# Pooled attention by couples of head pairs in 64x64 quadrants, the fifth local unit turned by DMA, in a fused attention and SoLU feed-forward kernel

## The chip, the cores and the metric

The kernel runs on one core of a Trainium2 chip. The time is the device time of one execution in microseconds (us); the time of a kernel is the median of its timed runs. A profile is taken in an execution of its own.

## The reference, cut to what matters

Eight batches of eight heads, 576 positions, 64 numbers a head. Two attentions are added: one over sequences pooled by 4 (144 positions), repeated four times, and one within a band of 3 positions to either side. Then comes a feed-forward layer with SoLU and a layer norm, over all 4608 positions.

```python
q_d = q.reshape(B, H, Sd, factor, D).mean(axis=3)        # k_d, v_d alike
out_up = np.repeat(sm_attn(q_d, k_d, v_d), factor, axis=2)
mask = np.abs(pos[:, None] - pos[None, :]) < factor
scores = np.where(mask, scale * np.matmul(q, k.transpose(0, 1, 3, 2)), -1000000000.0)
out_local = np.matmul(softmax(scores), v)
x = (out_up + out_local).transpose(0, 2, 1, 3).reshape(B * S, H * D)
h = x @ w_in                                             # 512 -> 1024
e = np.exp(h - h_max)
solu = h * e / (e.sum(-1) + 1e-9)
ln = (solu - mu) / np.sqrt(var + 1e-06) * g_ln
return ln @ w_out                                        # 1024 -> 512
```

## The kernel before

The work is cut into steps. Each piece is a generator (`steps`, `pair_steps`, `ffn_in`, ...) whose parts between two `yield`s are one step each. `plan` lists all steps, 2029 of them, and the list ORDER (lines 26 to 123) says in which order they are written into the program; the engines then run their instructions in that order, each in its own queue, and wait for each other by semaphores. A second list, OTHER, names steps whose element-wise operation goes to the other of two engines. All DMAs are issued by SyncE (SP), in order.

**Attention, a batch at a time.** q and k are loaded and turned to have the head's 64 numbers on partitions (two heads above each other: a pair of heads, four pairs). They are summed by four for the pooled attention (`sums`, line 418).

- *Local attention* takes ten windows of 64 positions, two of them in a unit, five units a batch. The scores `sc` (lines 607, 695) and the products with the values `xp` (lines 665, 753) are matmuls of 64 rows by 64 columns of the array. Between the two the weights have to be turned. `Local` does it on TensorE (`plt`, line 655) and copies the result out of PSUM (line 658). `PairOfLocals`, for batches 3 to 7 and units 0 to 3, does it by eight DMAs in blocks of 32 rows (`plT<-pl`, line 741) and a DVE transpose within blocks of 32 (line 746). Unit 4 is a `Local` in every batch.
- *Pooled attention* (`Pooled`, line 773) takes one pair of heads at a time. Scores `sd` (line 788) are six matmuls of 64 rows, 64 columns and 144 moving columns. The softmax runs over three thirds of 48 queries. `pdt` (line 823) turns the weights in twelve TensorE transposes, 64 rows by 72 columns; two copies take them out of PSUM (`pdT`, lines 830 and 833). `po` (line 844) are four matmuls with 72 keys on the rows. The result is added to x four times over (`accumulate`, line 574). The pooled values `vd` are summed from four loads of 72 rows by two additions each (`pooled_vsum`, line 484).

**Feed-forward, 36 tiles of 128 positions.** x is split into a high and a low part (`xh`, `xl`, `xhl`, line 1009); `ffn_in` multiplies with the split w_in (24 matmuls of 128x512, `h`, line 862), takes the maximum, the exponential, the product, the mean and the scale s (lines 870 to 926) and sends the result to DRAM (`u`); `ffn_back` reads it back in blocks, DVE turns it (`v`, line 963), ACT and POOL or DVE split it (`uh`, `ul`), and `ffn_out` makes the other 24 matmuls (`o`, line 990). These wide matmuls stand between the small ones of attention, wherever ORDER puts them.

Of the kernel before, what the change touches and what calls it, by code (L numbers as in the profile page):

```python
# [10 lines left out]
F32 = mybir.dt.float32  # L11
# [24 lines left out]
124 126 417 133 134 213 214 125 143 215 239 506 113 114 288 240 241 429 430 289 431 432 663 264  # L36
155 248 486 225 418 2 487 493 494 135 136 226 495 227 290 313 156 228 229 291 230 440 242 243
496 21 244 245 231 419 246 422 292 441 137 442 249 507 293 294 488 489 497 490 653 144 145 247
5 462 250 451 433 265 463 420 251 148 464 465 23 423 295 296 256 297 252 298 314 315 4 266 267
253 428 268 254 255 452 461 443 316 9 257 466 302 453 317 146 147 157 158 269 318 319 434 258  # L40
338 17 339 435 436 473 474 421 658 513 514 19 475 467 272 259 299 340 300 515 454 437 444 476
270 654 271 438 260 664 261 468 262 445 477 469 303 304 305 439 363 341 342 343 498 499 263 470
446 447 455 306 307 456 471 320 321 659 344 309 280 281 648 665 660 273 472 655 656 457 458 322
364 478 282 365 301 479 661 500 283 666 459 284 448 285 366 460 480 274 286 449 287 275 345 481
276 277 424 426 327 278 279 649 482 650 651 308 501 502 508 346 347 509 689 510 690 516 691 491
492 677 678 701 323 702 668 679 425 427 324 325 310 311 517 348 680 349 713 328 329 330 331 332
652 518 519 326 511 512 367 333 681 520 714 682 334 335 521 368 369 676 352 688 336 725 674 522
523 692 736 683 684 370 371 13 350 524 881 737 715 525 372 657 716 703 704 312 738 662 373 353
354 526 726 355 356 359 357 685 358 360 686 693 351 694 886 548 527 727 695 705 377 746 573 706
528 696 529 887 530 888 687 531 747 549 378 379 717 361 700 718 667 1139 728 889 550 551 532  # L50
533 697 698 374 669 552 882 707 891 748 375 598 675 739 599 380 381 699 766 876 767 553 719 708
554 709 768 384 710 711 574 769 892 337 756 740 555 883 884 556 537 382 383 670 557 712 923 362
562 672 893 720 757 894 741 742 743 758 877 724 534 376 535 940 900 671 770 878 879 729 575 576
577 578 880 385 386 538 579 539 885 540 541 580 542 906 907 908 909 730 910 731 911 581 582 600
721 601 912 913 558 387 759 760 543 544 545 559 1122 560 561 761 762 763 941 563 564 536 732
583 584 914 942 924 1127 733 925 926 927 915 565 566 602 546 587 890 744 567 568 749 750 928
734 623 722 603 904 1132 604 673 569 570 735 723 745 1123 751 1124 585 605 929 752 753 606 607
608 609 624 764 765 952 571 930 943 944 945 946 947 771 754 755 772 588 589 625 773 626 627 590
591 592 774 628 775 776 777 547 972 953 916 954 629 630 1117 973 594 610 778 901 895 931 586
1128 779 962 917 611 593 780 974 932 948 801 949 631 595 963 781 826 975 782 802 803 1125 964  # L60
804 783 612 955 922 956 632 633 1133 896 965 966 967 596 613 614 918 615 634 635 616 617 1129
933 934 1134 968 1135 805 1118 806 969 636 807 618 919 597 619 620 1130 905 572 935 902 784
1119 1120 982 983 984 920 897 921 827 828 985 637 950 638 639 621 903 951 898 936 1131 640 899
829 830 937 938 939 976 977 986 970 978 979 971 785 641 642 957 958 1165 980 959 1166 1167 808
786 1338 787 981 1168 809 643 987 790 1169 1170 1121 988 788 960 831 961 644 989 1147 832 1148
1149 1150 833 834 990 991 1171 1151 1152 851 1017 852 1333 791 1126 810 811 812 813 814 1193
1182 1334 792 1172 793 645 1173 1146 646 853 1335 1339 854 1348 1136 622 992 1018 815 794 795
797 855 647 1141 856 1153 857 816 817 835 1340 796 798 818 1194 993 994 789 836 1343 858 859
837 799 819 820 1183 821 1349 838 1184 1154 1195 1344 995 996 997 840 860 1137 822 823 1174
1175 1345 1346 998 1163 1138 865 841 842 843 1196 999 1042 1203 1336 839 800 1213 1214 1215  # L70
1204 1350 1341 861 1351 866 1143 1216 1155 1019 1020 1021 1156 1140 1157 1000 1001 1181 824 844
1205 845 846 1176 862 1363 1364 863 864 1067 1365 1584 1366 1367 1022 847 848 1574 1023 1398
1399 1381 867 1382 1217 1043 1044 1185 1068 1045 1337 868 869 849 1024 1144 1186 1187 1025 1368
1177 1178 1188 1400 1369 1383 1401 1206 1026 1207 850 1002 1027 1189 1384 1092 1046 1164 870
1003 1004 871 1370 1047 1385 1218 1028 1223 1352 1048 872 873 1006 1145 1219 1220 1069 1347
1208 1224 1158 1225 1159 1031 1386 1226 1070 1209 1210 1029 874 1007 1008 1049 1009 1160 1161
1361 1190 1032 1162 1191 1192 825 1197 1211 1227 1228 1371 1342 1142 1589 1093 1071 1010 1179
1180 1013 1011 1012 1372 1014 1033 1387 1034 1035 1229 1230 1030 1072 1212 1073 1050 1409 1362
1355 1373 1198 1231 1074 1199 1575 1075 1410 1411 1005 1051 1015 1585 1076 1056 1077 1094 1095
1402 1232 1200 1586 1587 1221 1412 1374 1375 1388 1222 1096 1376 1419 1036 1201 1439 1389 1202  # L80
# [1079 lines left out]
```

## Time and profile before

| | |
|---|---|
| timed runs (us) | 582.44, 582.76, 589.12; median 582.76 |
| span of the profiled execution | 587.5 us |
| granted TensorE clock, mean | 0.990 |
| busy: PE, DVE, ACT, POOL | 568.1, 472.5, 333.4, 298.9 us |
| DMA | 99.59 MB, q1 65.7% of 16 engines' time |

PE is TensorE's matmuls, PEld its weight loads, DVE is VectorE, ACT ScalarE, POOL GpSimd, SPq the queue of SyncE that issues DMAs. A name such as `pdt<-ident,pd` says which tile an instruction writes and which it reads. A form such as `64*72 64x64` says how many rows and columns of the array a matmul uses, and then the partitions and elements that it works on. A row of the timeline has the start and the length in us; the note in brackets is the idle time before it and what ended it. A busy time is the time in which any instruction of the group ran; since matmuls are pipelined, the length of one is more than its distance to the next. In groups by line, the columns are the busy time, the mean of one in ns, and the engine's idle time before, with what released it.

### The profile page before, as it was taken

Reading aid. Unit: us, or ns where it says so; the run is one execution under the profiler, and the core shown is the slowest. Engines: PE = TensorE matmul, PEld = TensorE weight load, DVE = VectorE, ACT = ScalarE, POOL = GpSimd, SP = SyncE. Lnnn points to the kernel's source line nnn. Section 1 sums busy time; section 2 is a strip of 40 time slices with the busy share of each in tenths; the row PEclk is TensorE's granted clock in tenths of the full one; section 3 lists DMA queues with packets and bytes.
Section 4 is the critical chain, followed back from the end, with each engine's and each line's share of the span. In section 5 each row is a group of like instructions: output and inputs, shape, how many; then the busy total and the mean of one; then the engine's idle time right before and its main releaser. Section 6 shows DMA issues by size and latency. Waiting matters only on the chain.

```text
span 587.5 us, 15257 instructions
## 1 busy us (share of the span) xinstructions
PE 568.1 (97%) x5852; PEld 437.2 (74%) x5852; DVE 472.5 (80%) x779; ACT 333.4 (57%) x750; POOL 298.9 (51%) x447
## 2 busy tenths in 40 slices
PE   7899989999999997999999999999999999999997
PEld 3676667777777775877777777777777777788875
DVE  7999999899898878897988876898879777644650
ACT  4788678468546644466475653457545664453452
POOL 3767588857373744358543455357431842433130
PEclk9999999999999996999999999999999999999999
DMA  8999767788877888577867887665666245314221
GB/s 279 288 218 229 169 140 183 196 183 172 220 160 183 187 197 181 154 167 180 180 152 198 222 197 192 155 192 152 177 190 133 91 142 164 113 44 167 89 91 54
DMA packets 207113, 99.59 MB, mean 170 GB/s; under 512 B 163136, under 2 KB 193344, under 8 KB 207040
## 3 DMA queue, kind: packets, MB, share of 16 engines
q1 hardware_dynamic: 207040, 98.61, 65.7%
q8 instruction: 46, 0.75, 0.6%
q14 instruction: 27, 0.22, 0.1%
HBM read 65.54 MB, written 27.79 MB: 159 GB/s over the span
## 4 chain that ended last, share of the span: by engine, by line
PE 72%; DVE 13%; DMA 4%; POOL 4%; ACT 3%; issue 2%; SPq 0%; DVEq 0%; ACTq 0%; POOLq 0%
PE o L990 30%; PE h L862 28%; PE po L844 2%; PE sc L695 2%; PE sd L788 2%; DMA v<-u 2%; PE xp L753 2%; PE pdt L823 2%; PE sc L607 1%; DVE nmx L870 1%; DVE w L375 1%; DVE e L877 1%; DMA vs<-in_v_dram 1%; PE plt L655 1%; DVE w L379 1%
## 5 line engine op out<-in xcount | busy, mean ns | idle before, releaser
L862 PE MATMUL h<-wi_h,xh 128*128 128x512 f32 x288 | 116.9, 406 | 1.4 <-DVE e L877 1.3
L990 PE MATMUL o<-wo_h,uh 128*128 128x512 f32 x288 | 117.4, 408 | 0.4 <-ACT osb L997 0.4
L862 PE MATMUL h<-wi_h,xl 128*128 128x512 f32 x288 | 114.4, 397 | 0.7 <-POOL xl L1024 0.7
L990 PE MATMUL o<-wo_l,uh 128*128 128x512 f32 x288 | 114.6, 398 | 0.0
L862 PE MATMUL h<-wi_l,xh 128*128 128x512 f32 x288 | 113.7, 395 | 0.0
L990 PE MATMUL o<-wo_h,ul 128*128 128x512 f32 x288 | 79.0, 396 | 0.0
L973 POOL TENSOR_TENSOR ul<-v,uh 128x512 fp32r<-128x512 f32 x40 | 51.8, 1296 | 43.6 <-ACT uh L970 35.5
L874 ACT ACTIVATE e<-h,nmx 128x1024 f32<-128x1024 f32 x36 | 40.1, 1114 | 47.1 <-DVE nmx L870 43.4
L862 PEld LDWEIGHTS h<-wi_h,xh 128*128 128x128 f32 x288 | 54.1, 188 | 16.7 <-issue 2.9
L990 PEld LDWEIGHTS o<-wo_h,uh 128*128 128x128 f32 x288 | 54.6, 189 | 15.8 <-issue 1.4
L862 PEld LDWEIGHTS h<-wi_h,xl 128*128 128x128 f32 x288 | 54.1, 188 | 15.3 <-POOL xl L1024 2.1
L990 PEld LDWEIGHTS o<-wo_h,ul 128*128 128x128 f32 x288 | 54.1, 188 | 13.4 <-DVE ul L973 0.3
L990 PEld LDWEIGHTS o<-wo_l,uh 128*128 128x128 f32 x288 | 54.7, 190 | 12.2
L870 DVE TENSOR_REDUCE nmx<-h 128x1 f32<-128x1024 f32 x36 | 43.7, 1215 | 24.8 <-PE h L862 24.8
L862 PEld LDWEIGHTS h<-wi_l,xh 128*128 128x128 f32 x288 | 54.1, 188 | 12.0
L877 DVE SCALAR_TENSOR_TENSOR e<-h,e 128x1024 f32<-128x1024 f32 x36 | 43.8, 1216 | 14.8 <-ACT e L874 14.7
L970 ACT ACTIVATE uh<-v 128x512 fp32r<-128x512 f32 x70 | 42.7, 624 | 20.7 <-issue 8.5
L963 DVE STREAM_TRANSPOSE v<-v 128x512 f32<-128x512 f32 x70 | 46.4, 688 | 4.2 <-DMA v<-u 4.1
L997 ACT ACTIVATE osb<-o,s 128x512 f32<-128x512 f32 x36 | 24.5, 681 | 40.4 <-PE o L990 24.8
L1024 POOL TENSOR_TENSOR xl<-x,xh 128x512 fp32r<-128x512 f32 (+1 forms) x26 | 32.6, 1256 | 22.3 <-ACT xh L1021 22.0
L487 POOL TENSOR_TENSOR vs<-vs 72x512 f32<-72x512 f32 x24 | 31.6, 1318 | 17.0 <-DMA vs<-in_v_dram 16.7
L882 POOL TENSOR_SCALAR nmu<-su 128x1 f32<-128x1 f32 x36 | 8.2, 228 | 59.8 <-DVE e L877 56.9
(128 smaller groups left out, 1124.0 us busy)
## 6 DMA issues: line engine op xcount, KB each, us to landing
u<-e SPq DMA_DIRECT2D x35, 512.0 KB
v<-u SPq DMA_DIRECT2D x140, 128.0 KB
vs<-in_v_dram SPq DMA_DIRECT2D x32, 288.0 KB
out_dram<-osb SPq DMA_DIRECT2D x36, 256.0 KB
qm<-in_q_dram SPq DMA_DIRECT2D x96, 72.0 KB
km<-in_k_dram SPq DMA_DIRECT2D x96, 72.0 KB
vw<-in_v_dram SPq DMA_DIRECT2D x80, 64.0 KB
vw<-in_v_dram SPq DMA_DIRECT2D x40, 128.0 KB
```

The source lines that it names most:

```text
L487: eng.tensor_tensor(out=vs[:, :, 0:2 * D], in0=vs[:, :, 0:2 * D], in1=vs[:, :, 2 * D:4 * D], op=ALU.add)
L695: nc.tensor.matmul(at[rows(wi), par, pr], bt.qT[rows(par), pr, s0:s0 + W], bt.kT[rows(par), pr, s0:s0 + W], start=True, stop=True,)
L862: nc.tensor.matmul(hps[:, n, :], src[:, cc, :], wt[:, cc, n * 512:(n + 1) * 512], start=(cc == 0 and src is xh and wt is wi_h), stop=(cc = ...
L870: nc.vector.tensor_reduce(out=nmx, in_=hf, op=ALU.max, axis=AX.X, negate=True)
L874: nc.scalar.activation(e, hf, AF.Exp, bias=nmx, scale=1.0, accum_out=se)
L877: nc.vector.scalar_tensor_tensor(out=e, in0=hf, scalar=1.0, in1=e, op0=ALU.mult, op1=ALU.mult, accum_out=su)
L963: nc.vector.transpose(vg, vg)
L970: nc.scalar.activation(uh, tp, AF.Copy)
L973: (usual if v is None else engine(usual, nc.vector)).tensor_tensor(out=ul, in0=tp, in1=uh.bitcast(F32), op=ALU.subtract)
L990: nc.tensor.matmul(o, src[:, j, :], wt[:, 4 * g + j, :], start=(g == 0 and j == 0 and src is uh and wt is wo_h), stop=(g == 1 and j == 3 a ...
L997: nc.scalar.activation(osb, o, AF.Copy, scale=s)
L1024: engine(nc.gpsimd, nc.vector).tensor_tensor(out=l, in0=src, in1=h.bitcast(F32), op=ALU.subtract)
```

## The change

The first 470 steps of ORDER stay. From there on both lists are new (the plan has 1868 steps), and four things change in what the steps do.

1. From batch 2 on (`COUPLED = 2`) `Couple` takes the place of `Pooled`: two pairs of heads, g and g + 2, are done together. Scores are twelve matmuls, as many as two pairs had, in an order that goes round all four quadrants of the array. The weights are turned by 36 plain matmuls with the identity, 48 x 48, instead of 2 x 12 transposes. po has three thirds of 48 keys, twelve matmuls of 48 rows instead of 2 x 4 of 72. Both pdT copies and both additions to x become one for two pairs. Values are loaded in three pieces of 112 rows, the heads 0 to 3 on the lower half and 4 to 7 on the upper.
2. Unit 4 of batches 3 to 7 is turned by eight DMAs and a DVE transpose like the other units: `PairOfLocals` becomes `ByTransfers`, for one unit or two.
3. From tile 7 on (`SHORT = 7`) the scale s of the layer norm is worked out from the sum of exponentials directly: one POOL operation more, three fewer, and no reciprocal on DVE.
4. Code for a way of summing values on TensorE, which was switched off, is gone.

```diff
+    COUPLED = 2
+    SHORT = 7
...
+    class Couple:
+        def steps(self):
+            prs = (g, g + 2)
+            sd = two_banks(*scores_bank(b, g), f"sd_{b}_{g}")[:, :, 0:QC * SD]
+            at = sd.rearrange("p a (c n) -> p a c n", c=QC)
+            for c in range(QC):
+                for a, pr in enumerate(prs):
+                    for par in range(2):
+                        nc.tensor.matmul(
+                            at[rows(par ^ a), a, c, :],
+                            qd_flat[rows(par), (NPR - 1 - pr) * SD + c * QN:][:, 0:64],
+                            bt.kd[rows(par), pr, :], start=True, stop=True,
+                        )
...
+            for k in range(KC):
+                for c in range(QC):
+                    for x, a in TILES:
+                        q_rows = slice(x * 64, x * 64 + QN)
+                        nc.tensor.matmul(
+                            to[a * 64:a * 64 + KN, x, k, c, :],
+                            pds[a][q_rows, c, k * KN:(k + 1) * KN], ident[q_rows, q_rows],
+                            start=True, stop=True,
+                        )
...
+            for k in range(KC):
+                for a in range(2):
+                    for par in range(2):
+                        keys = slice(a * 64, a * 64 + KN)
+                        nc.tensor.matmul(
+                            po[rows(par), a, :], bt.vd[keys, k, 2 * g + par, :],
+                            pdT[keys, par ^ a, k, :], start=k == 0, stop=k == KC - 1,
+                        )
...
+        if i >= SHORT:
+            nc.gpsimd.tensor_scalar(
+                out=se, in0=se, scalar1=se, scalar2=1e-6, op0=ALU.mult, op1=ALU.mult
+            )
...
+        if i >= SHORT:
+            m2 = small.tile([P, 1], F32, tag="m2", name=f"m2_{i}")
+            nc.scalar.activation(e0, e, AF.Square, accum_out=m2)
+            yield
+            nc.gpsimd.tensor_scalar(
+                out=m2, in0=m2, scalar1=1.0 / DFF, scalar2=se, op0=ALU.mult, op1=ALU.add
+            )
+            nc.gpsimd.tensor_tensor(out=s, in0=m2, in1=mhalf, op=ALU.pow)
...
-            local = [PairOfLocals(bt, 0, not late), PairOfLocals(bt, 2, not late), Local(bt, 4, not late)]
-        pooled = [Pooled(bt, pr, late) for pr in range(NPR)]
+            local = [
+                (ByTransfers(bt, u, n, not late), 16 if n == 2 else 12, range(u, u + n))
+                for u, n in ((0, 2), (2, 2), (4, 1))
+            ]
+        if bt.b < COUPLED:
+            pooled = [(Pooled(bt, pr, late), 10, ()) for pr in range(NPR)]
+        else:
+            pooled = [(Couple(bt, g), 12, ()) for g in range(2)]
```

How the two orders differ on TensorE after 768 wide matmuls (16 tiles' worth; batches 4 and 5 are under way). Before:

```order
L862 MATMUL h_4788<-wi_h,xl_4392 128x512
L844 MATMUL po_2_4820<-pdT_2_4428,vd_4025 64x144 x4
L753 MATMUL xp_0_4828<-plT_0_4681,vw_0_4583 64x64 x16
L788 MATMUL sd_1_4853<-kd_3810,qd_flat 64x144 x6
L844 MATMUL po_0_4863<-pdT_0_4747,vd_4025 64x144 x4
L788 MATMUL sd_3_4868<-kd_3810,qd_flat 64x144 x6
L990 MATMUL o_4951<-wo_h,uh_0_4700 128x512
```

Three kinds of small group alternate, and po (72 rows by 64 columns) uses the array in another form than xp and sd (64 by 64). In the changed kernel, at the same place and 24 wide matmuls earlier:

```order
L892 MATMUL pdt_1_4658<-ident,pd_1_0_4480 48x48 x2
L892 MATMUL pdt_1_4658<-ident,pd_1_1_4484 48x48 x2
L892 MATMUL pdt_1_4658<-ident,pd_1_0_4480 48x48
L912 MATMUL po_0_4695<-pdT_0_4489,vd_4326 64x144 x12
L930 MATMUL h_4729<-wi_h,xh_4491 128x512
...
L847 MATMUL sd_1_4759<-kd_4019,qd_flat 64x144 x12
L912 MATMUL po_1_4772<-pdT_1_4713,vd_4326 64x144 x12
```

One sd and one po now hold what two held, all of these groups lie within 64 by 64, and no group of another form stands between them. On SP, in the first batch that turns by DMA (batch 3), before:

```order
L741 DMA plT_0_2801<-pl_0_2573 32x512 x4
L286 DMA qm_2687<-in_q_dram 32x18x32 x4
L286 DMA km_2688<-in_k_dram 32x18x32 x4
L942 DMA v_3232<-u_2945 32x4x256 x4
L299 DMA vw_2_3239<-in_v_dram 64x8x64 x2
L910 DMA u_3243<-e_3039 128x1024
L316 DMA vs_0_0_3248<-in_v_dram 72x4x256
```

And now:

```order
L718 DMA plT_0_2970<-pl_0_2403 32x512 x4
L296 DMA vs_1_3077<-in_v_dram 64x4x256
L296 DMA vs_1_3077<-in_v_dram 48x4x256
L718 DMA plT_4_3080<-pl_110 32x256 x4
L1081 DMA out_dram<-osb_3052 128x512
L1024 DMA v_3168<-u_2966 32x4x256 x4
L982 DMA u_3229<-e_2978 128x1024
L718 DMA plT_4_3080<-pl_110 32x256 x4
```

The turning of unit 4 (`plT_4`) has moved into this queue, four issues for each of the two windows, among the loads of the values (`vs`, now two issues a piece) and the round trip of the feed-forward tiles (`u`, `v`).

More of the change, by code (lines that the diff above doesn't have):

```diff
@@ L225, in pooled_local_attention_then_solu_ffn @@
     nc.vector.memset(mhalf, -0.5)
-    GR = SD // 2
-    BAND = {0: (0, 16), 1: (3, 15), 3: (1, 15)}
-    bands = {}
-    def make_bands():
-        t = moe.tile([P, DFF], F32, tag="e", name="bands")[:, 0:3 * 160]
-        t = t.rearrange("p (r x) -> p r x", r=3)
-        nc.gpsimd.memset(t, 0.0)
-        by_half = ident.rearrange("p (h k) -> p h k", h=2)
-        for n, (r, (off, m)) in enumerate(BAND.items()):
-            nc.vector.tensor_reduce(
-                out=t[:, n, GR:GR + m],
-                in_=by_half[:, :, off:off + FAC * m].rearrange("p h (j i) -> p j h i", i=FAC),
-                op=ALU.add, axis=AX.XY,
-            )
-            bands[r] = t[:, n]
     LP = 2 * W + 2
@@ L312, in big, with load_halves @@
         return load.tile([P, 1024], F32, tag="big", name=name, bufs=6)
+    def load_halves(b, c):
+        vs = big(f"vs_{b}_{c}").rearrange("p (h x) -> p h x", h=H // 2)
+        for half, n in ((0, 64), (1, KN)):
+            src = v[b, half * (H // 2), c * KN * FAC, :]
+            nc.sync.dma_start(
+                vs[half * 64:half * 64 + n],
+                bass.AP(
+                    tensor=src.tensor, offset=src.offset,
+                    ap=[[FAC * D, n], [S * D, H // 2], [1, FAC * D]],
+                ),
+            )
+        return vs[0:ROOM]
     def load_vs(b, c, hs):
@@ L734, in steps @@
             yield
-            plT = big(f"plT_{b}_{u}")
+            if units == 2:
+                plT = big(f"plT_{b}_{u}")
+            else:
+                plT = wk.tile([P, NPR, 2, W], F32, tag="plT", name=f"plT_{b}_{u}")
+                plT = plT.rearrange("p r a w -> p (r a w)")
             half = N * 32
@@ L747, in steps @@
             yield
-            plT = plT.rearrange("p (a n h q) -> p n h a q", a=2, n=2, q=32)
-            for n in range(2):
+            plT = plT.rearrange("p (a n h q) -> p n h a q", a=2, n=units, q=32)
+            for n in range(units):
                 xp = two_banks(ps_a, "a", f"xp_{b}_{u + n}")
@@ L841, in steps @@
                 for par in range(2):
-                    parts = bt.value(kc, 2 * pr + par)
-                    for n, vt in enumerate(parts):
-                        nc.tensor.matmul(
-                            po[par * 64:par * 64 + 64, :], vt, pdT[:, kc, par * SD:(par + 1) * SD],
-                            start=(kc == 0 and n == 0), stop=(kc == 1 and n == len(parts) - 1),
-                        )
+                    nc.tensor.matmul(
+                        po[rows(par), :], bt.vd[:, kc, 2 * pr + par, :],
+                        pdT[:, kc, par * SD:(par + 1) * SD], start=kc == 0, stop=kc == 1,
+                    )
             yield
@@ L1057, in tile_in @@
         row(xhl(i), 2)
-        row(ffn_in(i), 12 if i not in ON_PE else 11)
+        row(ffn_in(i), (12 if i < SHORT else 10) - (i in ON_PE))
         if i not in ON_PE:
```

161 lines of the change are left out of this document (98 added, 63 removed), and 173 rows, old and new, of tables (ORDER, OTHER).

## The prediction

> **What bounds the kernel now.** I read the page first: the busy shares and the chain that ended last.
>
> ```profile
> span 587.5 us, 15257 instructions
> PE 568.1 (97%) x5852; PEld 437.2 (74%) x5852; DVE 472.5 (80%) x779; ACT 333.4 (57%) x750; POOL 298.9 (51%) x447
> PE 72%; DVE 13%; DMA 4%; POOL 4%; ACT 3%; issue 2%; SPq 0%; DVEq 0%; ACTq 0%; POOLq 0%
> ```
>
> TensorE is the bound by its share, but a share says nothing of stages. So next I asked for busy time in stretches, cut where the granted clock changes (columns: length, then PE, PEld, DVE, ACT and POOL busy with instruction counts, clock, DMA share, GB/s).
>
> ```profile
> 104.00:222.00 118.00, 116.18 (x1204) 89.50 (x1196) 102.17 (x166) 68.58 (x161) 70.81 (x104) 1.00 0.80 186
> 222.00:226.00 4.00, 1.14 (x22) 0.78 (x20) 4.00 (x5) 2.78 (x5) 2.06 (x4) 0.79 0.76 180
> 226.00:235.00 9.00, 8.97 (x102) 7.03 (x103) 7.03 (x11) 3.29 (x7) 2.49 (x4) 0.52 0.94 190
> 246.00:584.00 338.00, 336.41 (x2850) 264.30 (x2848) 252.79 (x407) 175.75 (x391) 152.00 (x257) 1.00 0.56 152
> ```
>
> PE idles 1.8 us in the first row, 2.9 in the second and 1.6 in the last: 6.3 us in all from 104 us on. The rest is matmul work. So a microsecond taken from PE is a microsecond of the end, as long as the others keep up. Rows two and three are one accident. At 0.79 of the clock for 4 us and 0.52 for 9 us, 4 x 0.21 + 9 x 0.48 = 5.2 us of clock were lost, and this came behind PE's longest wait:
>
> ```profile
> 220.03 3.79 DVE L490 TENSOR_TENSOR vd<-vs 72x256 f32<-72x256 f32 x1
> ```
> ```profile
> 226.03 0.38 PE L695 MATMUL sc<-kT,qT 64*64 64x64 f32 x4 [2.90 <-DVE pdT L265]
> ```
>
> A sum of values took 3.79 us on DVE, the copy of pdT behind it came late, and PE stood for 2.90 us. The span is 587.5 us and the median of the timed runs 582.76 us; the span less the 5.2 us of lost clock is 582.3 us. I take it that the timed median holds no half clock, and sum from 582.4 us.
>
> **The change part by part.** All its PE work is small matmuls between the wide ones, so their prices are wanted. In the timeline a group's price is the distance from its start to the next group's start. The form reads rows*columns of the array, then out rows x moving columns.
>
> ```profile
> 356.07 0.69 PE L753 MATMUL xp<-plT,vw 64*64 64x64 f32 x32
> 356.59 0.64 PE L665 MATMUL xp<-plT,vw 64*64 64x56 f32 x32
> 357.16 0.49 PE L990 MATMUL o<-wo_h,uh 128*128 128x512 f32 x1
> ```
> ```profile
> 428.04 0.60 PE L655 MATMUL plt<-ident,pl 128*128 128x128 f32 x4
> 428.57 0.53 PE L823 MATMUL pdt<-ident,pd 64*72 64x64 f32 x12
> 429.03 0.69 PE L753 MATMUL xp<-plT,vw 64*64 64x64 f32 x32
> 429.65 0.50 PE L990 MATMUL o<-wo_h,uh 128*128 128x512 f32 x1
> ```
>
> The same 32 records of xp cost 0.52 us where a group of the same 64*64 form follows, 0.57 where the form was there already but a full-width matmul follows, and 0.62 where both neighbours have another form. So entering a form costs 0.05 us, leaving it 0.10, and the work 0.47. A visit to a form costs 0.15 us. The 32 records are 16 matmuls of the program (each plain fp32 matmul stands as two records, the transposes of pdt as one). 16 matmuls in 0.47 us are eight steps of two, 0.058 us a step: the two halves of the rows work at once, two quadrants at a time and not four. And 56 columns cost no less than 64.
>
> ```profile
> 316.29 0.71 PE L844 MATMUL po<-pdT,vd 72*64 72x144 f32 x8
> 316.93 0.69 PE L753 MATMUL xp<-plT,vw 64*64 64x64 f32 x32
> ...
> 318.04 0.71 PE L844 MATMUL po<-pdT,vd 72*64 72x144 f32 x8
> 318.68 0.71 PE L788 MATMUL sd<-kd,qd_flat 64*64 64x144 f32 x12
> 319.32 0.50 PE L990 MATMUL o<-wo_h,uh 128*128 128x512 f32 x1
> ```
> ```profile
> 263.99 1.20 PE L788 MATMUL sd<-kd,qd_flat 64*64 64x144 f32 x24
> 265.12 0.50 PE L862 MATMUL h<-wi_h,xh 128*128 128x512 f32 x1
> ```
>
> po (four matmuls, 72 rows, so no halves) costs 0.64: less the visit 0.49, or 0.122 us for a matmul of 144 columns. sd (six matmuls) costs 0.64, less the visit 0.49; two of them in a row 1.13, less the visit 0.98. That is eight steps of 0.122 for twelve matmuls, where perfect pairs would need six.
>
> Now the sum, 24 pairs of heads (batches 2 to 7) against 12 couples:
> - Scores sd: 24 x 0.49 = 11.8 us. A couple's twelve matmuls alternate the halves of the rows in the order that sc and xp have, so I take six steps: 12 x 6 x 0.122 = 8.8. Saved 3.0 (nothing, if they take eight).
> - Turning pdt: 0.46 (428.57 to 429.03), less the visit 0.31; 24 x 0.31 = 7.4. A couple has 36 plain matmuls of 48 columns in alternating quadrants, 18 steps at 0.058: 12 x 1.04 = 12.5. Lost 5.1.
> - Values po: 24 x 0.49 = 11.8. A couple has twelve matmuls of 144 columns, but in the order of rows low, low, high, high. No group of before has that order. Bounds: six steps as in sc (8.8) and twelve, one after the other, as in po now (17.6). Nearest is sd, which also repeats a half and needs eight: 12 x 8 x 0.122 = 11.7. Saved 0.1, with -5.8 to +3.0 as the ends.
> - Turning the last local unit on PE goes in batches 3 to 7:
>
> ```profile
> 91.47 0.60 PE L655 MATMUL plt<-ident,pl 128*128 128x128 f32 x4
> 91.82 0.48 PE L862 MATMUL h<-wi_h,xh 128*128 128x512 f32 x1
> ```
>   0.35 us each, 5 x 0.35 = 1.8 saved.
> - Forms: pdt and po each had a form of their own (64*72, 72*64); now every small group but the plt has 64*64. I counted the visits in the order of PE from where the two orders part: 109 before, 49 after. 60 x 0.15 = 9.0 saved. This is the largest term, and none of it stands in the change's arithmetic.
>
> In all 3.0 - 5.1 + 0.1 + 1.8 + 9.0 = 8.8 us less on PE.
>
> The 48 columns are where a rule speaks against the change. The Trainium skill (TensorEngine Tiling (Array Packing), Instruction Overhead) says that each matmul carries some 60 cycles, so that one of free size 1 takes as long as one of 60. The trace agrees for 56 columns (0.57 us, the price of 64 with the exit). By that rule pdt costs 12.5 us as summed; priced by the column it would be 48/64 of it, 9.4, and the sum 11.9.
>
> Off PE, each edit is covered by PE's own time:
>
> ```profile
> L263 ACT ACTIVATE pdT<-pdt 72x288 f32<-72x288 f32 x49 | 18.3, 400 | 34.4 <-PE pdt L823 27.3 <-DVE pdT L265 4.9 <-PE po L844 2.2
> L874 ACT ACTIVATE e<-h,nmx 128x1024 f32<-128x1024 f32 x36 | 40.1, 1114 | 47.1 <-DVE nmx L870 43.4 <-DVE rsd L810 3.4
> L916 POOL TENSOR_TENSOR va<-r 128x1 f32<-128x1 f32 x36 | 9.5, 263 | 54.9 <-DVE r L913 42.3 <-ACT uh L970 8.0 <-DVE rsd L810 4.5
> ```
>
> A couple's copy of pdT has 864 elements in a row; between the 400 ns of 288 and the 1114 of 1024 that is about 960 ns, against two of 400 before: some 0.15 us more for each couple and engine, on engines with a fifth or more of their time free. The shorter statistics from tile 7 on drop one small DVE and two net small POOL operations a tile (263 ns for one): 29 x 0.5 = 15 us of POOL, hidden before behind PE, so worth nothing in the sum; it only loosens the supply. The values are summed in three pieces of 112 rows instead of four of 72 a batch, a third of it saved on POOL at most, hidden likewise. The transfers of the last unit add eight DMA issues and a DVE transpose a batch, which has to wait for them; in one such place the transposes of v and the ul of the second product stand behind it on DVE, and the o matmuls wait for those. A late landing there would reach PE; I count none, since DVE is free a fifth of the time, and leave the issues to the rival on SP's queue.
>
> 582.4 - 8.8 = 573.6, so **574 us**, with as much idling as before.
>
> **The rivals.** *The supply also gets better.* The 6.3 us of PE's idle time go, po runs in perfect pairs (2.9 more): 573.6 - 6.3 - 2.9 = 564, and half of that gives 569. For it: POOL alone sheds the 15 us of statistics, and nearly half of the idle time is the one wait of 2.90 us behind an operation that took 3.79 us. Against it: waits sit wherever an order is tight, this order is new behind step 470, and as many sums of values stand on DVE as before (eight).
>
> *Four quadrants at once.* If a couple's matmuls ran four at a time, sd and pdt would need half their steps and save 4.4 + 6.2 us, po three steps instead of eight, 7.3 us: 573.6 - 17.9 = 556 us. Against it stand the rows of xp: 16 matmuls in four quadrants take eight steps, not four. I give it little. The Trainium skill (TensorEngine Tiling (Array Packing), Key Properties) says that tiles work independently of each other, and its list of modes has four of 64x64. By that rule the time is this rival's; the trace agrees with two at a time, not four.
>
> *SyncE's queue becomes the bound, and the end is slower.* It issues every transfer, in order:
>
> ```profile
> 400.81 2.54 SPq L741 DMA_DIRECT2D plT<-pl  x4
> 403.44 3.73 SPq L999 DMA_DIRECT2D out_dram<-osb  x2
> 407.22 2.93 SPq L286 DMA_DIRECT2D qm<-in_q_dram  x4
> 410.20 2.12 SPq L286 DMA_DIRECT2D km<-in_k_dram  x4
> 412.42 0.44 SPq L910 DMA_DIRECT2D u<-e  x1
> 412.96 2.24 SPq L942 DMA_DIRECT2D v<-u  x4
> 415.24 5.24 SPq L299 DMA_DIRECT2D vw<-in_v_dram  x4
> ```
>
> Rows end within 0.1 us of the next: the queue is full for 20 us. An issue of plT costs 0.64 us (2.54/4); 40 more are 25 us over five batches, 5 us a batch. While there is slack on SP this is hidden: PE idles 1.6 us in all of 246 to 584, full queue or not. It decides once q and k of the next batch, queued behind the new issues, land after their transposes are due. If all 25 us came onto PE, 573.6 + 25 = 599; if half, 586.
>
> **How the numbers follow.** Two per cent, about what a measurement of this kernel can tell from no change, is 11.7 us: below 571.1 or above 594.4. Forecast as summed (571 to 580, po between its ends): 0.60. Better supply (564 to 571): 0.25. Four quadrants: 0.03. SP's queue (586 to 599): 0.12, of which less than half lies above 594.4. Faster by over 2%: 0.25 + 0.03 and 0.02 from the forecast's edge, 0.30; slower 0.05; within 0.65. The range: at the low end the better supply, 566; at the high end po one after the other (579.5) with one accident like that of 222 us (2.9 + 5.2), or half of SP's case: 587.
>
> **What would show it.** A couple's sd near 0.73 us and its pdt near 1.04 where groups of the same form stand on both sides; its po between 0.73 and 1.46, which settles its order of rows; PE's idle time from 104 us on near 6 us. Wrong, if PE idles over 12 us, if its waits name transfers of q, k or plT, or if a couple's group costs by the quadrant or by the record.

## The result, and the profile after

| | before | changed |
|---|---|---|
| timed runs, median (us) | 583.47 | 588.75 |
| lowest to highest | 581.68 to 589.12 | 587.08 to 594.75 |
| ratio to before, 95% interval | | 1.0091 [1.0069, 1.0113] |

The changed kernel is slower by 0.9%, within the 2% of "no change", and 14.8 us above the forecast of 574. The ratios, here and below, are to the kernel before as it was timed beside each kernel, and leave out executions in a slower state. A timed run is the span plus 1.7 us, so the profiled execution of before (587.5) is the timed one of 589.12. The prediction took the span for the time and left the wait of 2.9 us in it; these two slips nearly cancel (587.5 + 1.7 - 2.9 - 5.2 = 581.1), and its start of 582.4 lies 1.1 us below the median.

The page of the changed kernel, its span and the busy times:

```profile
span 586.3 us, 16418 instructions
PE 557.8 (95%) x6504; PEld 433.3 (74%) x6504; DVE 471.4 (80%) x714; ACT 327.0 (56%) x706; POOL 285.0 (49%) x378
```

TensorE did get less to do: 557.8 us busy against 568.1. The other engines are busy no longer than before. Yet the span did not follow, so the time must be between the instructions. The stretches, cut where the granted clock changes (length, then PE, PEld, DVE, ACT, POOL busy, clock, DMA share, GB/s):

```profile
104.00:205.00 101.00, 98.79 (x1250) 78.47 (x1251) 89.77 (x138) 59.39 (x129) 60.45 (x89) 1.00 0.80 189
205.00:210.50 5.50, 2.50 (x66) 1.78 (x68) 5.04 (x8) 4.95 (x18) 5.17 (x7) 1.00 1.07 273
210.50:214.00 3.50, 3.50 (x28) 2.71 (x20) 3.44 (x4) 1.76 (x3) 2.46 (x3) 0.51 0.86 137
214.00:404.00 190.00, 184.49 (x2132) 145.60 (x2131) 158.61 (x225) 94.90 (x193) 90.29 (x115) 1.00 0.77 189
404.00:408.50 4.50, 1.87 (x41) 1.58 (x36) 3.83 (x6) 2.00 (x5) 1.52 (x4) 1.00 0.13 37
408.50:412.00 3.50, 3.50 (x10) 2.69 (x10) 3.40 (x8) 3.50 (x11) 0.63 (x2) 0.51 0.00 0
412.00:584.00 172.00, 169.85 (x1548) 135.11 (x1546) 111.81 (x157) 85.03 (x175) 56.64 (x90) 1.00 0.42 131
```

From 104 us on, PE idles 480.0 - 464.5 = 15.5 us, against 6.3 before. 3.0 and 2.6 us of it lie in the two short rows at 205 and 404, and behind each of these stands a stretch of half clock, 1.7 us lost in each. The other 9.9 us are spread over shorter waits, which are not followed up here. The prediction had named over 12 us as its refutation.

The groups of a couple, from the timeline of the changed kernel:

```profile
313.60 0.97 PE L847 MATMUL sd<-kd,qd_flat 64*64 64x144 f32 x24
314.39 0.92 PE L912 MATMUL po<-pdT,vd 48*64 48x144 f32 x24
315.23 0.50 PE L1072 MATMUL o<-wo_h,uh 128*128 128x512 f32 x1
...
285.23 0.99 PE L892 MATMUL pdt<-ident,pd 48*48 48x48 f32 x72
286.09 0.96 PE L847 MATMUL sd<-kd,qd_flat 64*64 64x144 f32 x24
```

Start to next start: sd 0.79, po 0.84 with 0.10 for leaving the form, pdt 0.86. Most po ahead of a wide matmul took 0.90, so a po costs some 0.8 us without the exit. Against the forecast sd is 0.06 dearer, and po and pdt are cheaper. What got worse is the supply. DVE's waits for transfers from 104 us on, in the changed kernel and, in the second fence, before:

```profile
DVE v L1045 <- DMA v<-u: 11.5, 7, 4.9
DVE plT L723 <- DMA qm<-in_q_dram: 5.0, 1, 5.0
DVE plT L723 <- DMA plT<-pl: 3.7, 3, 1.7
```
```profile
DVE v L963 <- DMA v<-u: 4.1, 3, 2.1
```

The columns are the sum, the number of waits and the longest. With some shorter waits DVE stands 22.7 us for transfers, against 5.1.

**One stall, followed back.** The wait at 205 us. ACT has a tile e ready at 190.18 + 1.14 = 191.3 us; SyncE issues its transfer u only at 197.43, behind the values, four plT, the output and v:

```profile
190.18 1.14 ACT L972 ACTIVATE e<-e,nmu 128x1024 f32<-128x1024 f32 x1
...
202.94 1.06 ACT L986 ACTIVATE e<-e 128x1024 f32<-128x1024 f32 x1 [4.77 <-DMA u<-e]
```
```profile
190.96 1.30 SPq L296 DMA_DIRECT2D vs<-in_v_dram  x2
192.36 2.42 SPq L718 DMA_DIRECT2D plT<-pl  x4
194.88 0.53 SPq L1081 DMA_DIRECT2D out_dram<-osb  x1
195.50 1.83 SPq L1024 DMA_DIRECT2D v<-u  x4
197.43 0.38 SPq L982 DMA_DIRECT2D u<-e  x1
```
```profile
205.77 0.40 PE L930 MATMUL h<-wi_h,xl 128*128 128x512 f32 x1
208.94 0.90 PE L730 MATMUL xp<-plT,vw 64*64 64x64 f32 x32 [2.77 <-ACT pd L868]
```

The sum of squares at 202.94 overwrites e in place, so it must wait until u has read e: 4.77 us in which ACT's queue stands. The exponentials of the next couple (pd) come late for it, and PE waits 2.77 us. Two readings offer themselves. *Theory A*: the shorter statistics take the square two steps sooner, and its wait (13.9 us in all) is the loss. *Theory B*: SyncE's queue is the loss, and the square is only one of the places where its lateness is felt. *Theory C*: neither, the new order is just tighter for DVE and ACT.

### The profile page after: what moved, and what is told of

Same layout as the page of the kernel before. It is cut to its first block, busy times and chain, and to the rows that moved or that the text cites. A ratio compares the mean times of both kernels' runs of the same rounds, so it can differ in the third digit from the quotient of the medians.

```text
span 586.3 us, 16418 instructions
## 1 busy us (share of the span) xinstructions
PE 557.8 (95%) x6504; PEld 433.3 (74%) x6504; DVE 471.4 (80%) x714; ACT 327.0 (56%) x706; POOL 285.0 (49%) x378
## 3 DMA queue, kind: packets, MB, share of 16 engines
q1 hardware_dynamic: 210240, 101.11, 66.9%
## 5 line engine op out<-in xcount | busy, mean ns | idle before, releaser
L1055 POOL TENSOR_TENSOR ul<-v,uh 128x512 fp32r<-128x512 f32 x37 | 49.2, 1331 | 38.9 <-ACT uh L1052 38.0
L930 PEld LDWEIGHTS h<-wi_h,xl 128*128 128x128 f32 x288 | 54.4, 189 | 14.8 <-POOL xl L1106 1.6
L1052 ACT ACTIVATE uh<-v 128x512 fp32r<-128x512 f32 x70 | 43.2, 624 | 37.9 <-DVE v L1045 26.9
L930 PEld LDWEIGHTS h<-wi_l,xh 128*128 128x128 f32 x288 | 54.5, 189 | 12.5
L1072 PEld LDWEIGHTS o<-wo_l,uh 128*128 128x128 f32 x288 | 54.7, 190 | 11.9
L1045 DVE STREAM_TRANSPOSE v<-v 128x512 f32<-128x512 f32 x70 | 47.2, 691 | 11.5 <-DMA v<-u 11.5
L988 POOL TENSOR_SCALAR m<-m,se 128x1 f32<-128x1 f32 x29 | 14.1, 486 | 58.6 <-ACT e L986 58.5
L1079 ACT ACTIVATE osb<-o,s 128x512 f32<-128x512 f32 x36 | 24.5, 680 | 28.7 <-PE o L1072 12.4
```

The source lines that it names most:

```text
L930: nc.tensor.matmul(hps[:, n, :], src[:, cc, :], wt[:, cc, n * 512:(n + 1) * 512], start=(cc == 0 and src is xh and wt is wi_h), stop=(cc = ...
L988: nc.gpsimd.tensor_scalar(out=m2, in0=m2, scalar1=1.0 / DFF, scalar2=se, op0=ALU.mult, op1=ALU.add)
L1045: nc.vector.transpose(vg, vg)
L1052: nc.scalar.activation(uh, tp, AF.Copy)
L1055: (usual if v is None else engine(usual, nc.vector)).tensor_tensor(out=ul, in0=tp, in1=uh.bitcast(F32), op=ALU.subtract)
L1072: nc.tensor.matmul(o, src[:, j, :], wt[:, 4 * g + j, :], start=(g == 0 and j == 0 and src is uh and wt is wo_h), stop=(g == 1 and j == 3 a ...
```

## The experiments

Sixteen kernels. In the table, "tile to u" is the time from the end of the operation that makes a tile to the issue of its u<-e, a mean over the 16 to 18 tiles between 150 and 400 us, worked out from the timeline: how late SyncE's queue is. "DVE stands" is for transfers, from 104 us on. The last column is from the first o matmul (`o<-wo_h,uh`) to the last of this kind, which leaves the start out. The profiled execution of before holds the accident at 222 us (2.9 + 5.1 us) in its 493.4; without it, 485.4. All but the time and the ratio come from one execution of each kernel; those of e9 and e12 (582.6 and 581.4 us) were 3 to 4 us shorter than their medians, that of e11 was at its median.

| | issues | time, us | ratio to before | tile to u | DVE stands | first o | first to last o |
|---|---|---|---|---|---|---|---|
| before | 668 | 583.5 | | 4.3 | 5.1 | 88.6 | 493.4 |
| changed | 710 | 588.8 | 1.009 [1.007, 1.011] | 5.4 | 22.7 | 90.8 | 490.2 |
| e1 square later | 710 | 597.9 | 1.023 [1.019, 1.027] | 5.1 | 23.7 | 88.9 | 498.1 |
| e2 last unit on PE | 680 | 585.3 | 1.001 [0.999, 1.004] | 4.0 | 15.0 | 91.2 | 487.2 |
| e3 output by ACT | 674 | 591.9 | 1.013 [1.009, 1.017] | 3.5 | 11.9 | 92.7 | 491.9 |
| e4 before, more issues | 708 | 601.6 | 1.030 [1.025, 1.034] | 5.8 | 15.3 | 92.7 | 502.6 |
| e5 fewer q, k issues | 614 | 573.8 | 0.980 [0.972, 0.988] | 3.6 | 10.7 | 88.4 | 478.4 |
| e6 before, fewer q, k issues | 572 | 581.7 | 0.996 [0.992, 1.001] | 2.1 | 1.0 | 89.3 | 485.4 |
| e7 square and sum later | 710 | 590.8 | 1.010 [1.006, 1.015] | 5.7 | 29.9 | 89.4 | 493.2 |
| e8 u sooner | 710 | 630.9 | 1.078 [1.070, 1.086] | 2.0 | 62.8 | 89.7 | 533.9 |
| e9 heads regrouped | 630 | 585.7 | 1.003 [1.000, 1.006] | 2.9 | 9.4 | 96.2 | 479.3 |
| e10 by four | 582 | 603.2 | 1.032 [1.028, 1.036] | 2.4 | 19.4 | 102.9 | 491.0 |
| e11 q, k first | 630 | 585.6 | 1.004 [1.001, 1.007] | 2.5 | 7.9 | 100.5 | 477.9 |
| e12 and last unit on PE | 600 | 585.2 | 1.001 [0.998, 1.005] | 2.4 | 7.4 | 96.8 | 477.7 |
| e13 weights by two queues | 622 | 617.8 | 1.054 [1.049, 1.059] | 3.0 | 11.9 | 130.3 | 482.1 |
| e14 start by two queues | 618 | 621.1 | 1.061 [1.056, 1.065] | 2.8 | 11.8 | 134.7 | 480.5 |
| e15 weights later | 630 | 587.6 | 1.005 [1.002, 1.008] | 2.5 | 12.1 | 100.4 | 482.5 |
| e16 weights later still | 630 | 586.2 | 1.001 [0.998, 1.005] | 2.8 | 11.5 | 99.9 | 481.9 |

(Issues are counted in the profiled execution; e3's, e13's and e14's are SyncE's alone.)

### The square, taken later (e1, e7)

```diff
 e1:         if i >= SHORT:
-            nc.scalar.activation(e0, e, AF.Square, accum_out=m2)
             yield
+            nc.scalar.activation(e0, e, AF.Square, accum_out=m2)
             nc.gpsimd.tensor_scalar(out=m2, in0=m2, ...)
 e7: as e1, and in ffn_out, ahead of the scaling of osb:
+            nc.gpsimd.tensor_scalar(out=m2, in0=m2, ...)
+            nc.gpsimd.tensor_tensor(out=s, in0=m2, in1=mhalf, op=ALU.pow)
```

> Changed kernel, with the sum of squares (the activation that overwrites tile e) taken one plan step later, in the last step of the short statistics; nothing else. In the changed kernel ACT stands 13.9 us in this instruction until the transfer u<-e has read e, against 0.0 us before, and the longest of these waits (4.8 us at 198 us) comes just before PE's 2.8 us wait at 206 us and a stretch of half clock. Theory A (this wait on ACT is the loss): ACT's wait for u<-e falls to 3 us or less, PE's long waits behind ACT and DVE go, PE's idle time falls from 28.5 us towards 19 us, and the time from 588.8 to about 582 us. Theory B (SyncE's queue, fuller by 40 issues, is the loss): the wait on ACT may fall, but the time stays within 1.5 us of 588.8.

> Changed kernel with the sum of squares one plan step later and GpSimd's two operations behind it (m and its power) moved to just before the scaling of the output, so that GpSimd no longer stands for the square as it did in the first experiment. Theory A (ACT's wait of 13.9 us for u<-e is the loss): 580 to 584 us. Theory B (SyncE's queue): ACT's wait falls to 5 us or less and GpSimd's wait for the square (58 us) goes, yet the time stays within 586 to 591 us since DVE still stands 20 us for transfers.

The wait for u<-e in the changed kernel, in e1 and in e7, and what GpSimd then stood for in e1 and ACT in e7, from the chains of waits:

```profile
ACT e L986 <- DMA u<-e: 13.9, 6, 4.8
```
```profile
ACT e L987 <- DMA u<-e: 5.0, 3, 2.1
...
POOL m L988 <- ACT e L987: 107.2, 23, 14.7
```
```profile
ACT osb L1086 <- POOL s L1084: 25.5, 12, 4.4
```

ACT's wait fell from 13.9 to 5.0 us in e1 (4.5 in e7) and the time rose: 597.9 and 590.8. In e1 the square shares a step with GpSimd's operation behind it, GpSimd stands 107 us for it instead of 58.5, and what is queued on GpSimd behind it comes late; e7 took that away and made ACT stand 25.5 us for s in its place. Each removed one wait and made another, so neither isolates the square. But in both DVE stood for transfers as long as in the changed kernel or longer (23.7 and 29.9 us), and taking most of the square's wait away did not bring the time back. That speaks against theory A as the whole cause; e5 has to decide.

### Issues off SyncE's queue and onto it (e2, e3, e4)

```diff
 e2:
-        if b >= PAIRED:                # in load_vw
+        if b >= PAIRED and u < 4:
-                for u, n in ((0, 2), (2, 2), (4, 1))
+                for u in (0, 2)
+            ] + [(Local(bt, 4, not late, pad=True), 12, (4,))]
 e3:
-        nc.sync.dma_start(out[i * P:(i + 1) * P, :], osb)
+        nc.scalar.dma_start(out[i * P:(i + 1) * P, :], osb)
 e4, in the kernel before:
+                        for part in range(2 if u == 0 else 1):
+                            n = half // 2 if u == 0 else half
                             nc.sync.dma_start(plT[...][:, 0:n], pl[...][:, 0:n])
```

> Changed kernel, with one part undone: the last local unit of batches 3 to 7 is turned by TensorE again, as before, so that 40 plT issues (some 25 us of SyncE's queue) and five DVE transposes go, and five plt groups of 0.35 us on PE (1.8 us and their form visits) come back. An empty step keeps the order's numbers. Theory B (SyncE's queue): waits of DVE for plT, qm and v fall, PE's idle time falls by about 10 us, the time goes from 588.8 to 579 to 583 us. Theory A (the wait of the square on ACT): the work comes back on PE and nothing is won, 589 to 592 us.

> Changed kernel, with the 36 transfers of the result to DRAM issued from ACT's queue instead of SyncE's; nothing else. It takes 36 issues of 1.9 us, 67 us in all, off SyncE's queue, more than the 25 us that the change put there, and changes nothing on PE or DVE. Theory B (SyncE's queue): later transfers land sooner, waits of DVE for plT and v halve, and the time falls to 580 to 584 us, unless the issues cost ACT as much. Theory A (the wait of the square on ACT): u<-e is issued a little sooner, so a part of 13.9 us may go, but the time stays between 585 and 591 us.

> Kernel before, with the plT transfers of the first pair of units of batches 3 to 7 each split in two halves: 40 more issues on SyncE's queue at the same bytes, and nothing else. Theory B (SyncE's queue): the kernel before loses what the change lost beyond its PE work, 583.5 goes to 589 to 595 us, with PE's idle time up by 5 to 10 us. Theory A (the wait of the square on ACT): no change, 582.5 to 584.5 us.

e2 and e4 point the same way. Undoing the 40 plT issues (30 net, since the values' loads get ten more) gained 3.5 us although it gave PE 1.8 us back; that is less than expected, and most of the loss stayed. e4 is a strong sign: the kernel before, with the same bytes in 40 more issues and no other edit, goes from 583.5 to 601.6, more than any theory had asked for. It is not the queue's length alone there: the same plT now waits for 16 issues instead of 8. Half clock enlarges the loss: e4's profile holds 20.5 us of it, which cost some 10 us.

e3 is a miss for theory B. It took 36 issues off SyncE (20.0 us of issuing in the changed kernel, not the 67 of the expectation), tile to u fell to 3.5 us and DVE's standing to 11.9, as theory B wants, and the time was 3.2 us worse. So these two figures do not give the time by themselves. The output's issue now sits in ACT's own queue, and ACT in e3 stands 26.4 us for transfers from 104 us on (22.6 in the changed kernel), 16.4 of it in waits that name loads of values, q and k. That the relief was paid for in ACT's queue fits this, but no run shows it alone.

### Half as many issues for q and k (e5, e6)

```diff
-                for dh in range(2):
-                    Q = 2 * par + dh
-                    nc.sync.dma_start(t[nm][Q * 32:Q * 32 + 32, pr], ...)
+                nc.sync.dma_start(
+                    t[nm][rows(par), pr],
+                    bass.AP(..., ap=[[32, 64], [32 * D, 18], [1, 32]]),
+                )
```

> Changed kernel, with q and k of batches 2 to 7 loaded by half as many transfers of twice the size: 96 issues (some 50 us) off SyncE's queue, the same bytes and the same number of pieces, and the same work on every other engine. This changes what is computed: within a head the rows of q and k are read in another order and overlapping, so the output is not the reference's. Theory B (SyncE's queue holds the transfers up): a finished tile waits less for its u<-e to be issued (5.4 us on average from 150 to 400 us in the changed kernel, 4.3 before), DVE's waits for transfers fall well below 22.7 us, PE's idle time goes back to 18 or 20 us, and the time falls from 588.8 to 574 to 580 us, the PE gain of the change. Theory A (the wait of the square on ACT): a part of it goes with the sooner u<-e, 584 to 588. If the order itself is too tight for DVE (theory C), 584 or more with DVE's waits for transfers gone.

> Kernel before with the same edit as the run ahead of this one: 96 issues off SyncE's queue by loading q and k of batches 2 to 7 with half as many transfers of twice the size (other rows of q and k are read, so the output is not the reference's). Theory B: the kernel before hardly stands for transfers (5.1 us on DVE), so it gains little, 579 to 583 us, and the changed kernel with this edit beats it by the 8 to 12 us that PE's work shrank by. Theories A and C: the same here, but the changed kernel stays level with this one or behind.

573.8 us: the changed kernel gains 15.0 us, the kernel before 1.7. The two pages, e5 and then e6:

```profile
span 572.1 us, 16310 instructions
PE 551.4 (96%) x6504; PEld 430.3 (75%) x6504; DVE 471.4 (82%) x714; ACT 327.7 (57%) x706; POOL 282.9 (49%) x378
```
```profile
span 580.3 us, 15143 instructions
PE 563.8 (97%) x5852; PEld 434.2 (75%) x5852; DVE 470.7 (81%) x779; ACT 332.8 (57%) x750; POOL 298.7 (51%) x447
```

Both ran at full clock but for the last 2 us, so the two PE sums compare the work alone: 563.8 - 551.4 = 12.4 us less (10.3 between before and changed, each with half clock in it). With the relief in both, the changed kernel is ahead by 581.7 - 573.8 = 7.9 us, not by the 12.4: PE still idles 572.1 - 551.4 = 20.7 us in e5, against 16.5 in e6. The stall of 205 us is gone. The same tile in e5, ACT and SyncE:

```profile
187.47 1.14 ACT L971 ACTIVATE e<-e,nmu 128x1024 f32<-128x1024 f32 x1
...
194.65 1.06 ACT L985 ACTIVATE e<-e 128x1024 f32<-128x1024 f32 x1 [0.60 <-DMA u<-e]
```
```profile
188.56 1.83 SPq L1023 DMA_DIRECT2D v<-u  x4
190.50 0.38 SPq L981 DMA_DIRECT2D u<-e  x1
```

From the tile to its u 1.9 us instead of 6.1, and the square, at its old place, waits 0.60 instead of 4.77. This decides between A and B: the time fell into B's range and not into A's, although ACT still stands 9.1 us for u<-e in all of e5 (13.9 in the changed kernel). Theory C falls for most of the loss too, since the order is untouched; the 4.5 us that stay behind PE's gain may be its part, and no run parts them. One part of the expectation was wrong: the issues became longer, and SyncE's issuing time fell by 10 us (413 to 403), not by 50. What fell is the lateness: tile to u from 5.4 to 3.6 us, and DVE's standing from 22.7 to 10.7. Both are about those of e3, but ACT stands only 14.2 us for transfers here, against 26.4 there. The DMA engines were no emptier (68.8% of their time against 66.9%), so bandwidth is not what was won; whether it is the count of issues or the time of certain ones stays open.

One wait did not go: the one of 2.6 us at 404 us in the changed kernel, which e5 has too (at 391.8). There v stands behind eight plT in the order itself, SyncE, DVE and PE of the changed kernel:

```profile
381.73 5.01 SPq L718 DMA_DIRECT2D plT<-pl  x8
386.84 0.53 SPq L982 DMA_DIRECT2D u<-e  x1
387.46 4.41 SPq L1024 DMA_DIRECT2D v<-u  x8
```
```profile
392.51 1.31 DVE L1045 STREAM_TRANSPOSE v<-v 128x512 f32<-128x512 f32 x2 [4.94 <-DMA v<-u]
```
```profile
407.33 0.47 PE L930 MATMUL h<-wi_h,xh 128*128 128x512 f32 x1 [2.63 <-DVE e L945]
```

DVE stands 4.94 us, has hardly a gap from then on, and 15 us later frees the PSUM of h too late.

### The queue is in order (e8)

```diff
         if i not in ON_PE:
-            yield
             away[i] = dram.tile([P, DFF], F32, tag="u", name=f"u_{i}")
             nc.sync.dma_start(away[i], e)
+            yield
         yield
```

> Changed kernel with u<-e issued one plan step sooner (in the step that makes it), so that it takes an earlier place in SyncE's queue; the queue has as many issues as before. Theory B: the queue is in order, and what comes sooner for u comes later for the rest and SyncE stands for e at times: 585 to 592 us. Theory A: the square finds u<-e done, its wait falls from 13.9 to 5 us or less, and the time falls to 581 to 585 us.

630.9 us, far beyond both expectations, though in the direction of theory B's. SyncE and DVE of e8:

```profile
114.27 2.12 SPq L264 DMA_DIRECT2D km<-in_k_dram  x4
127.35 0.34 SPq L981 DMA_DIRECT2D u<-e  x1
127.80 0.38 SPq L1024 DMA_DIRECT2D v<-u  x1
```
```profile
132.88 0.71 DVE L1045 STREAM_TRANSPOSE v<-v 128x512 f32<-128x512 f32 x1 [5.55 <-DMA v<-u]
```

SyncE stands from 116.4 to 127.3 us until e is there, and nothing else is issued. One plan step sooner for u costs every transfer behind it; DVE then stands 62.8 us. It also explains why u could not simply be moved up.

### The same relief with the reference's data (e9 to e16)

With heads pr and pr+4 in a pair, two pairs' q or k are one even stretch of DRAM:

```diff
 e9:
+        pr -= pr % 2                   # load_q_k, once for two pairs
-                        t[nm][Q * 32:Q * 32 + 32, pr], ...
+                        t[nm][Q * 32:Q * 32 + 32, pr:pr + 2] ...,
+                        bass.AP(..., offset=src[b, pr + 4 * par].offset + dh * 32,
+                                ap=[[D, 32], [32 * D, 2 * NB], [1, 32]]),
-            nc.sync.dma_start(hl, self.src[n])
+                for par in range(2):   # w_in: rows of heads cc and cc + 4
+                    nc.sync.dma_start(hl[rows(par)], w_in[r:r + 64, ...])
 e10: four pairs at once        e11: e9, ORDER begins with 24 25, then 33 32 sooner
 e12: e11 and e2                e13: e9, second half of hl by nc.scalar
 e14: e13, second half of batch 0's vs by nc.scalar
 e15, e16: e9, the first steps of Weights up to 13 or 23 places later in ORDER
```

> Changed kernel with 96 issues off SyncE's queue and the reference's output: the two heads of a pair are now pr and pr+4 (before 2pr and 2pr+1), so that two pairs' q or k lie in one even stretch of DRAM and come with one transfer of twice the size per group of 32 rows. The rows of the first weight matrix, the values and a couple's pairs follow that order (24 more issues in the first two batches and the weights). Theory B (SyncE's queue): as in the run that only halved these issues, 572 to 577 us, faster than the changed kernel and the kernel before. Theory C (the new order itself is too tight for DVE): 584 or more.

> As the run ahead of this one, with all four pairs' q or k in one transfer per group of 32 rows: another 48 issues fewer, each transfer four times the first size. Theory B: as fast or up to 3 us faster (571 to 577 us), the less the more of the queue's lateness is gone already; if the larger transfers hold up the ones behind them on the DMA engines, slower by a few us.

> The kernel of the regrouped heads (96 issues fewer for q and k), with the loads of the first two pairs' q and k put ahead of the weights at the very start; the rest of the order is kept. In the regrouped kernel the first q came 4 us later behind the split weight loads, PE stood 3.1 us at 13.4 us, and the first o matmul came at 96.2 us against 90.8 in the changed kernel and 88.4 in the run with half the q and k issues. If theory B is right and only this start ate the gain: 575 to 580 us, faster than the kernel before (584.5). If the start is not the cause: 584 to 587 us as the regrouped kernel.

> As the run ahead of this one, with the last local unit of batches 3 to 7 turned by TensorE again: another 40 issues off SyncE's queue and 1.8 us of plt groups back on PE. Theory B: if the queue is still late, 572 to 577 us; if the 96 issues were enough, PE's added work shows, 1 to 3 us slower than the run ahead of this one.

> The kernel of the regrouped heads (96 issues fewer for q and k), with the second half of each weight load of the first product issued from ACT's queue. If the 8 us were lost to the split weight loads at the start: the first o matmul comes at 89 to 92 us instead of 96.2 and the time falls to 576 to 580 us. If the regrouping costs by itself: 584 to 587 us.

> As the run ahead of this one, with the second half of the first batch's value loads issued from ACT's queue as well. If the start is the cause: 575 to 579 us. If ACT stands for the buffers of these loads: up to 5 us slower than the run ahead of this one.

> The kernel of the regrouped heads with the first weight loads and their conversions moved some 15 places later in the order, behind the first q and k. From the first o matmul to the end the regrouped kernel took 10 us less than the changed kernel; if the start comes back to 90 us, the time is 576 to 580 us. If weights come too late for the first h matmuls, the first o matmul stays at 96 us or later and the time at 585.

> As the run ahead of this one, with the weights some 30 places later. Either sooner still for q and k (575 to 579 us) or, if the weights are late for the first h, slower than the run ahead of this one by some us.

Read by the time, all eight miss: none beats the kernel before, and e9 and e11 came out where their expectations put the other reading (584 or more). The last column, which the expectations of e9 and e10 do not name, agrees with theory B for all but e10. From the first o matmul to the last, e9, e11 and e12 take 477.7 to 479.3 us, as e5 (478.4), and e13 to e16 480.5 to 482.5, against 490.2 in the changed kernel: 8 to 12 us less with this data too, in these single executions. In whole times e9, e11 and e12 gain only 3 to 4 us on the changed kernel. What they lose, they lose before the first o matmul, which comes at 96 to 101 us (103 in e10, 130 and later in e13 and e14) instead of 89 to 91. There the weights take eight more issues and the first values eight more, and neither q first (e11) nor weights later (e15, e16) won that back; each only moved PE's waits of 2 to 4 us, and with them the half clock, to another place within the first 100 us. That the added issues cause the late start is likely, but not shown. No version with the reference's output is faster than the kernel before.

e13 and e14 answered another question, ACT of e13:

```profile
13.68 0.47 ACTq L361 DMA_DIRECT2D stage<-in_moe_w_in_dram  x1
23.31 0.66 ACT L372 ACTIVATE w<-stage 128x512 f32<-128x512 f32 x1 [10.24 <-DMA stage<-in_moe_w_in_dram]
```

ACT issues this load only when its own queue has come to it, at 13.68 us, and the copy of the same data, next on ACT, stands 10.24 us until the load is there; ACT's copies for PE stand behind it. The first o matmul comes 34 us later than in e9. e10 shows the other limit, SyncE of e10:

```profile
347.43 2.41 SPq L735 DMA_DIRECT2D plT<-pl  x4
349.94 4.82 SPq L271 DMA_DIRECT2D qm<-in_q_dram  x4
354.81 7.30 SPq L271 DMA_DIRECT2D km<-in_k_dram  x4
362.14 3.43 SPq L735 DMA_DIRECT2D plT<-pl  x4
```

Fewer issues still, but 12.1 us of q and k in one block between two halves of a unit's plT; PE's wait of 5.9 us at 362.9 us lies there; it ends at an xp, which needs plT, though the trace names no releaser. Only some 2 of the 14 us that e10 takes longer than the changed kernel come behind the first o matmul.

## Why the prediction was wrong

**What bounds the kernel: right for the kernel before.** PE is still the busiest engine, at 95%, but what was taken from it no longer came off the end.

**The prices of PE: the direction right, three sizes off.** sd runs in six steps, as taken (0.79 with 0.06 for the change of group). po nearly does too: its order of rows low, low, high, high pairs about as well as the alternating one (0.79 us at the least, some 0.8 as a rule), so the lower bound held and not the eight steps (1.03). pdt costs 0.86, 0.045 to 0.048 us a step and not 0.058, if its 36 matmuls go two at a time as taken. Here row and rule part: by the 60 cycles of the Trainium skill (TensorEngine Tiling (Array Packing), Instruction Overhead) 48 columns should have cost as much as 60, an estimate of 0.054 us a step from the 0.058 of 64 columns. The runs are nearer to 48/64 of 0.058, which is 0.044. With these prices the sum is 24 x 0.49 - 12 x 0.79 = 2.3 for sd, 2.3 for po, 12 x 0.86 - 7.4 = 2.9 lost on pdt, 1.8 and 9.0 as before: 12.5 us saved instead of 8.8, and e6 less e5 measures 12.4. The form visits are the largest term; that they were real rests on this agreement, since no run changes them alone.

**"With as much idling as before": the step that failed.** It rests on two sentences: "I count none, since DVE is free a fifth of the time", and that SyncE's full queue "is hidden", since PE idled little behind it. Both read a share as slack. DVE works in order: a fifth of free time is no help to what stands behind v for 5 us, and it stood 22.7 us for transfers instead of 5.1. And a full queue behind which PE idled 1.6 us in 338 was a queue just in time. e4 shows how near the edge it was: 40 issues alone cost the kernel before 18 us. In numbers: 583.5 - 12.4 = 571.1 us was to be had, and 588.8 was measured, 17.7 more. PE's idle time is 12.0 us of it (28.5, against 19.4 - 2.9 = 16.5 before without its accident) and half clock 5.1.

**The rival had the right queue, and the right time in part by luck.** "SyncE's queue becomes the bound" stood at 586 to 599, chance 0.12; the measured 588.75 lies in it. But it added its loss to 573.6 us, where PE's true saving leads to some 571, so 17.7 us were lost, not the 15 that this time means in its sum. Its 25 us for 40 plT issues is exact (49.2 us for 80 before, 74.0 for 120 after, summed from the timeline). It missed the values: three pieces of two loads each take 27.9 us with batches 0 and 1, against 14.0 before, so that SyncE's issuing time went from 382 to 413 us. And the point from which it decides was misplaced. It was less q and k that came late for their transposes (1.8 us of DVE's waits) than what stands behind them: u, v and plT. Its price was a share of the issuing time; in fact the time is lost where DVE or ACT stands, in a few long waits and many short ones.

**Half clock, priced only at the end of the range.** The forecast held none, the upper bound one accident. Each of the two long waits took another 1.7 us by the clock, and a third such stretch lies at 29.6 us. Of the 15.0 us between the changed kernel and e5, 28.5 - 20.7 = 7.8 us are idle time of PE and 5.1 half clock (557.8 busy less 551.4 holds it).

**"It only loosens the supply": wrong.** GpSimd's busy time did fall by 14 us (298.9 to 285.0), but not by the 15 us of statistics: their operations after the mean took 65.2 us before and 61.5 after, since the fewer operations run longer (m 0.49 us, where 0.26 was taken for one). The sums of values made the difference, 51.6 us before and 37.9 after. The shorter statistics also brought the square nearer to the transfer that reads its tile, which made it one of the places where the lateness is felt.

## What to carry to other kernels

Price every DMA that an edit adds on the queue that issues it, and judge slack not by how busy that queue is or how little the bound engine waits behind it, but by how long a finished tile lies before its transfer is issued, and by how long the other engines stand for transfers (e3 shows that the first alone is not enough). Adding a few issues to the unchanged kernel (as e4) tells in one run whether there is a margin. An engine that is free a fifth of its time but works in order may have no slack for a late landing. A wait that is removed can come back elsewhere while its source, here the queue, is late (e1, e7); relieve the source in both kernels and compare.

## What the runs showed of the hardware

- Half clock came in stretches of 3.4 us or multiples: 3.4 three times in the changed kernel, 10.2 before, 6.8 in e1, one of 6.8 and two of 10.2 in e10. The waits of PE ahead of them were 1.4 to 5.9 us long (1.7, 2.8 and 2.6 in the changed kernel), and the clock fell 1 to 4 us after they began; a wait of 2.6 us in e5 was followed by none. The Trainium skill (TensorE: Matmul & The Clock Gate, What's actually happening) has a free-running window of 3413 ns, which fits the lengths, and an idle window as the condition; here waits shorter than a window were enough.
- Half as many loads of twice the size were worth 15 us where the queue was late (e5); a quarter as many of four times the size, with the heads regrouped (e10), came out 14 us over the changed kernel, 12 of them before the first o matmul. The Trainium skill (DMA: Bandwidth & Descriptors, Issuing engines are not separate DMA queues) calls the issue time that a second issuing engine saves usually small beside the DMA. Here issuing takes 413 of 586 us on SyncE, and yet a second queue was no cure: 3 us slower in e3, 32 slower than e9 in e13, where the issue stands in ACT's own order.
- Four matmuls whose rows go low, low, high, high run nearly two at a time, like alternating ones (po, 0.79 us at the least for twelve, against 0.79 for sd's twelve).
